# Attention's first query block as one chunk of 128 keys, and the order of logits and result transposes

## The chip, the cores and the metric

The kernel runs on one core of a Trainium2 chip. The metric is the device time of one execution in microseconds (us). A core has TensorE (PE in the profile; its weight loads are PEld), VectorE (DVE), ScalarE (ACT), GpSimd (POOL) and SyncE (SP), which here issues most of the loads and stores. Every engine runs its own queue in the order in which the program was written.

## The reference

Three stages follow one another; only the first is touched by the change.

```
scores = scale * q @ k^T            # batch 4, heads 8, 768 positions, 64 per head
keep   = first 8 keys, or the 96 keys up to the query
scores = where(keep, scores - slope[h] * dist, -1e9)
a      = exp(scores - max);  a = a / (sum(a) + 1e-9)
x      = (a @ v)                    # to 3072 tokens x 512
x      = x + gate * expert(x)       # 8 experts, top 1, only where x @ w_skip > 0
out    = experts by capacity, 384 tokens each (greedy by logits x @ w_gate)
```

## The kernel before

**Attention.** Work goes by batch `b` (4), by pair of heads `hp` (4 each) and by `j` (3), a group of two query blocks of 128 rows, so 16 head pairs of three groups. The loop over `g` is a pipeline written by hand: in one turn it emits the exponentials of group g+2 (`e_stage`), the product with V of group g-1 (`o_stage`), a task or two from the list `todo`, the scaling of group g+1 (`n_stage`), the transposes of probabilities of group g (`t_stage`), the transposes of K and Q of a later pair (`qk_t`) and the scores of group g+3 (`s_stage`).

Only the keys that can count are used: query block i > 0 sees 232 keys (96 before its block, its own 128, the first 8), block 0 sees its own 128. Keys lie on partitions for the product with V, and 232 are more than 128, so every block's keys are split in two by their parity: the exponential writes them de-interleaved (`p r k -> p k r`), and the transposes, the copies and the products with V run over two chunks of half the keys. Block 0 is treated in the same way, with two chunks of 64. V is loaded to match: `vw` for the later blocks, `v0` (the name `v` in the rows) for the first 128 keys, with two neighbouring rows of V on one partition.

Names of tiles: `pb` probabilities, `pP` a bank of PSUM (five rotate) for transposes and more, `pts` the copy of transposed probabilities, `pO` the product with V, `xT` the attention's result with features on partitions, `xs` its transposed copy that is written to memory as `xd` and `x2d`, `pS` scores, `sb` scores with bias, `st` their maxima and sums.

**What stands in `todo`.** After each group but a pair's first, `x_stage` transposes half a pair's result (three transposes). After the last pair of a batch come also `logits` (four products of `xT` with the weights `wc` into `pP`, copied by ScalarE to the single tile `ls`) and `logits_t` (three transposes of `ls`, reduced by VectorE to `LG`). A turn of the loop takes one task, and a second if any is left. When the last batch is done, `route1` ranks the tokens for the first experts; the same routing of earlier batches runs beside the attention, in small VectorE instructions. What is left of `todo` is emitted behind the loop, with work on the expert weights (`ww`) between.

**Experts.** The expert stages follow, from a table of planned costs (`Clock`). They take the rest of the time and are not touched; their instructions and their order stay as they are.

Every operation is recorded through one helper, so all rows of the trace carry its line, L132; pieces are told apart by their tiles.

Of the kernel before, what the change touches and what calls it, by code (L numbers as in the profile page):

```python
# [7 lines left out]
F32 = mybir.dt.float32  # L8
# [162 lines left out]
def tile_attn_moe_moe(ctx: ExitStack, tc: tile.TileContext, q, k, v, n_global, n_local,  # L171
# [93 lines left out]
    def load_v(b, hp):  # L265
        w = VW[b, hp] = ld.tile([KP, NI - 1, 2, 2, D], F32, name="vw", bufs=3)
        z = V0[b, hp] = ld.tile([64, 2, 2, D], F32, name="v0", bufs=3)
        vv = v[b, 2 * hp:2 * hp + 2].rearrange("h (i x) d -> h i x d", x=128)
        nc.sync.dma_start(z.rearrange("p h r d -> p h (r d)"),
                          vv[:, 0].rearrange("h (p r) d -> p h (r d)", r=2))  # L270
        for h in range(2):
            def part(p0, p1, src):
                nc.sync.dma_start(w[p0:p1, :, h].rearrange("p i r d -> p i (r d)"),
                                  src.rearrange("i (p r) d -> p i (r d)", r=2))
            part(W // 2, KP - G // 2, vv[h, 1:])
            part(0, W // 2, vv[h, :NI - 1, 128 - W:])
            part(KP - G // 2, KP, vv[h, 0:1, :G].to_broadcast([NI - 1, G, D]))
# [62 lines left out]

    NG = NI // 2
    GR = [(b, hp, j) for b in range(B) for hp in range(HP) for j in range(NG)]
    SB = {}
# [4 lines left out]
    def s_stage(g):  # L348
# [11 lines left out]
        for x in range(2):  # L360
            i = 2 * j + x
            SB[g, x] = sb = wk.tile([128, 2, KW], F32, name="sb", bufs=4)
            for h in range(2):
                nc.vector.tensor_tensor_reduce(sb[:, h, :keys(i)], p_s[i, h][:, :keys(i)],
                                               (bias1 if i else bias0)[:, 2 * hp + h, :], 1.0, 3e38,
                                               op0=OP.add, op1=OP.min, accum_out=st[:, 0, x, h:h + 1])

    def e_stage(g, x, h):
        n = keys(2 * GR[g][2] + x)
        if h == 0:  # L370
            PB[g, x] = wk.tile([128, 2, 2, KP], F32, name="pb", bufs=6)
        nc.scalar.activation(PB[g, x][:, h, :, :n // 2].rearrange("p r k -> p k r"),
                             SB[g, x][:, h, :n].rearrange("p (k r) -> p k r", r=2), AF.Exp,
                             bias=ST[g][:, 0, x, h:h + 1], scale=-1.0, accum_out=ST[g][:, 1, x, h:h + 1])
        if h == 1:
            SB.pop((g, x))

    def n_stage(g):
# [3 lines left out]
        for x in range(2):  # L382
            n = keys(2 * GR[g][2] + x)
            for h in range(2):
                p = PB[g, x][:, h, :, :n // 2]
                nc.gpsimd.tensor_scalar(p, p, st[:, 2, x, h:h + 1], 1.0, op0=OP.mult, op1=OP.mult)

    def t_stage(g, x):
        n = keys(2 * GR[g][2] + x) // 2
        pt = ps.tile([128, 2, 2, 128], F32, name="pP", bufs=5)  # L390
        p = PB.pop((g, x))
        for h in range(2):
            for r in range(2):
                nc.tensor.transpose(pt[:n, h, r, :], p[:, h, r, :n], ident)
        PT[g, x] = wk.tile([128, 2, 2, 128], F32, name="pts", bufs=3)
        nc.vector.tensor_copy(PT[g, x][:n], pt[:n])

    def o_stage(g):
        b, hp, j = GR[g]
        po = ps.tile([128, 2, 128], F32, name="pO")  # L400
        for x in range(2):
            i = 2 * j + x
            n = keys(i) // 2
            t = PT.pop((g, x))
            for r in range(2):
                for h in (1, 0):
                    vv = VW[b, hp][:, i - 1, h, r, :] if i else V0[b, hp][:, h, r, :]
                    nc.tensor.matmul(po[h * 64:(h + 1) * 64, x, :], vv, t[:n, h, r, :], start=r == 0, stop=r == 1)
        if b not in XT:
# [448 lines left out]
    for g in range(-3, NU + 1):  # L858
# [28 lines left out]
        for i in (2 * j, 2 * j + 1):  # L887
            beside(b, hp, i)
        if j:
            todo.append((x_stage, (b, hp, j - 1)))  # L890
            if hp == HP - 1:
                todo.append((logits, (b, j - 1)))
                todo.append((logits_t, (b, j - 1)))
# [1172 lines left out]
```

## Time and profile before

| | |
|---|---|
| median of 3 runs | 776.23 us (775.8 to 778.62) |
| profiled execution | 777.47 us |
| span of its trace | 775.7 us |
| TensorE busy | 744.8 us, 96% |
| VectorE, ScalarE, GpSimd busy | 68%, 52%, 60% |
| transfers | 145370 packets, 132.23 MB, 170 GB/s |

The span is from the first to the last instruction of the profiled execution; its time, with what lies around, is 1.8 us more. Busy shares are means over stages with different limits, so the stage of the change has to be read by itself. Matmuls overlap in the pipeline: what one costs in a dense stretch is seen from start to start, not from the duration of one.

### The profile page before, as it was taken

Reading aid. Unit: us, or ns where it says so; the run is one execution under the profiler, and the core shown is the slowest. Engines: PE = TensorE matmul, PEld = TensorE weight load, DVE = VectorE, ACT = ScalarE, POOL = GpSimd, SP = SyncE. Lnnn points to the kernel's source line nnn. Section 1 sums busy time; section 2 is a strip of 40 time slices with the busy share of each in tenths; the row PEclk is TensorE's granted clock in tenths of the full one; section 3 lists DMA queues with packets and bytes.
Section 4 is the critical chain, followed back from the end, with each engine's and each line's share of the span. In section 5 each row is a group of like instructions: output and inputs, shape, how many; then the busy total and the mean of one; then the engine's idle time right before and its main releaser. Section 6 shows DMA issues by size and latency. Waiting matters only on the chain.

```text
span 775.7 us, 17432 instructions
## 1 busy us (share of the span) xinstructions
PE 744.8 (96%) x5910; PEld 628.7 (81%) x5910; DVE 526.1 (68%) x1952; ACT 403.3 (52%) x936; POOL 468.2 (60%) x821
## 2 busy tenths in 40 slices
PE   7999999899889999999999999999999999999997
PEld 5887777677659999999888677878788878788986
DVE  5987988979556676777634586778787778752110
ACT  5887787887547655555652113434333434255221
POOL 4664456755214464555793636975768777689911
PEclk9999999999999999999999999999999999999999
DMA  8686988897716766777760035626262636366311
GB/s 192 167 213 167 248 232 200 222 231 199 236 27 213 265 198 195 252 234 224 210 220 33 19 91 191 209 91 222 77 204 84 230 108 206 125 195 185 121 41 41
DMA packets 145370, 132.23 MB, mean 170 GB/s; under 512 B 65427, under 2 KB 112787, under 8 KB 145280
## 3 DMA queue, kind: packets, MB, share of 16 engines
q1 hardware_dynamic: 136896, 111.19, 48.9%
q0 software_dynamic: 6784, 19.51, 7.4%
q8 instruction: 48, 0.79, 0.4%
q10 hardware_dynamic: 1600, 0.39, 0.2%
q14 instruction: 42, 0.34, 0.1%
HBM read 108.80 MB, written 22.79 MB: 170 GB/s over the span
## 4 chain that ended last, share of the span: by engine, by line
PE 44%; POOL 8%; issue 6%; DMA 5%; DVE 4%; ACT 3%; POOLq 0%; DVEq 0%; ACTq 0%; SPq 0%
PE py L132 19%; PE ph L132 19%; POOL wl L132 7%; DMA wr<-in_moe_w_dram 4%; PE pr L132 3%; PE pt L132 3%; ACT wh L132 2%; DVE wl L132 1%; POOL out_dram L132 1%; DMA xg<-x2d,ids 1%; DVE py L132 1%; ACT ya L132 0%; DVE h L132 0%; POOL xg L132 0%; DVE o L132 0%
## 5 line engine op out<-in xcount | busy, mean ns | idle before, releaser
L132 POOL TENSOR_TENSOR wl<-wr,wh 128x256 fp32r<-128x256 f32 x356 | 253.6, 745 | 62.0 <-ACT wh L132 61.3
L132 ACT ACTIVATE wh<-wr 128x1024 fp32r<-128x1024 f32 (+1 forms) x148 | 142.2, 985 | 42.8 <-DMA wr<-in_moe_w_dram 26.8
L132 PE MATMUL py<-wh,h 128*128 128x512 f32 (+1 forms) x448 | 155.9, 401 | 0.0
L132 ACT ACTIVATE h<-ph 128x208 fp32r<-128x208 f32 (+2 forms) x132 | 54.4, 415 | 180.7 <-PE ph L132 168.3
L132 POOL TENSOR_SCALAR pb<-pb,st 128x232 f32<-128x232 f32 (+1 forms) x192 | 83.4, 453 | 74.3 <-ACT pb L132 24.2
L132 ACT ACTIVATE pb<-sb,st 128x232 f32<-128x232 f32 (+1 forms) x192 | 113.8, 664 | 10.1 <-DVE st L132 9.8
L132 DVE SCALAR_TENSOR_TENSOR h<-ph,h 128x208 fp32r<-128x208 f32 (+1 forms) x128 | 58.8, 460 | 88.8 <-ACT h L132 88.7
L132 PE MATMUL ph<-xh,wh 128*128 128x208 f32 (+1 forms) x512 | 99.1, 310 | 1.4 <-DVE h L132 1.4
L132 PE MATMUL ph<-xh,wl 128*128 128x208 f32 (+1 forms) x512 | 100.0, 311 | 0.0
L132 PE MATMUL ph<-xl,wh 128*128 128x208 f32 (+1 forms) x512 | 99.0, 311 | 0.0
L132 PEld LDWEIGHTS py<-wh,h 128*128 128x128 f32 (+1 forms) x448 | 82.0, 185 | 14.1
L132 PE MATMUL py<-wl,h 128*128 128x512 f32 (+1 forms) x224 | 90.9, 406 | 0.0
L132 PEld LDWEIGHTS ph<-xh,wh 128*128 128x128 f32 x512 | 82.2, 190 | 6.8 <-DVE h L132 1.6
L132 PEld LDWEIGHTS ph<-xl,wh 128*128 128x128 f32 x512 | 78.9, 190 | 1.1 <-issue 1.0
L132 PEld LDWEIGHTS ph<-xh,wl 128*128 128x128 f32 x512 | 78.9, 190 | 0.5 <-issue 0.3
L132 DVE TENSOR_TENSOR wl<-wr,wh 128x1024 fp32r<-128x1024 f32 x47 | 61.0, 1304 | 15.3 <-ACT wh L132 15.2
L132 DVE CUSTOM_DVE_ANT_0 sb<-pS,bias 128x232 f32<-128x232 f32 (+1 forms) x192 | 61.4, 374 | 8.9 <-PE pS L132 7.6
L132 DVE COPY pts<-pP 116x512 f32<-116x512 f32 (+1 forms) x96 | 60.7, 672 | 7.6 <-PE pP L132 7.1
L132 POOL DMA_INDIRECT xg<-x2d,ids x24 | 23.8, 990 | 52.2 <-DVE ids L132 19.1
L132 PE MATMUL pS<-kt,qt 64*128 64x232 f32 (+1 forms) x384 | 50.7, 382 | 1.0 <-ACT pb L132 1.0
L132 PE MATMUL pP<-ident,pb 128*116 128x128 f32 (+1 forms) x384 | 51.3, 277 | 0.0
L132 PE MATMUL pO<-pts,vw 116*64 116x128 f32 x640 | 46.3, 281 | 4.0 <-DVE pts L132 3.2
(465 smaller groups left out, 1267.5 us busy)
## 6 DMA issues: line engine op xcount, KB each, us to landing
wr<-in_moe_w_dram SPq DMA_DIRECT2D x136, 512.0 KB
xd<-xs SPq DMA_DIRECT2D x32, 192.0 KB
x2d<-xs SPq DMA_DIRECT2D x32, 192.0 KB
kraw<-in_k_dram SPq DMA_DIRECT2D x30, 192.0 KB
qraw<-in_q_dram SPq DMA_DIRECT2D x30, 192.0 KB
vw<-in_v_dram SPq DMA_DIRECT2D x32, 160.0 KB
vw<-in_v_dram SPq DMA_DIRECT2D x32, 120.0 KB
xT<-in_moe_w_dram SPq DMA_DIRECT2D x1, 1536.0 KB
```

Of the source, the lines that this page charges most:

```text
L132: r = f(*a, **k)
```

## The change

Query block 0 takes its 128 keys as one chunk. Its exponential writes them in one run, a new function `probs` gives the piece of `pb` that holds them, its transposes are one of 128 columns for each head in place of two of 64, the copy to `pts` has 256 elements on 128 partitions in place of 512 on 64, its product with V runs once over 128 rows for each head in place of twice over 64, and V's first block is loaded with one row of 64 numbers (256 bytes) for each partition and head in place of two (512 bytes). The later blocks' `pt` only changes the order of its two inner indices. Apart from that, `logits` goes into `todo` ahead of `x_stage`.

```diff
--- before.py
+++ after.py
@@ -264,10 +264,9 @@
 
     def load_v(b, hp):
         w = VW[b, hp] = ld.tile([KP, NI - 1, 2, 2, D], F32, name="vw", bufs=3)
-        z = V0[b, hp] = ld.tile([64, 2, 2, D], F32, name="v0", bufs=3)
+        z = V0[b, hp] = ld.tile([128, 2, D], F32, name="v0", bufs=3)
         vv = v[b, 2 * hp:2 * hp + 2].rearrange("h (i x) d -> h i x d", x=128)
-        nc.sync.dma_start(z.rearrange("p h r d -> p h (r d)"),
-                          vv[:, 0].rearrange("h (p r) d -> p h (r d)", r=2))
+        nc.sync.dma_start(z, vv[:, 0].rearrange("h p d -> p h d"))
         for h in range(2):
             def part(p0, p1, src):
                 nc.sync.dma_start(w[p0:p1, :, h].rearrange("p i r d -> p i (r d)"),
@@ -339,6 +338,7 @@
 
 
     NG = NI // 2
+    PTS = 3
     GR = [(b, hp, j) for b in range(B) for hp in range(HP) for j in range(NG)]
     SB = {}
 
@@ -365,12 +365,20 @@
                                                (bias1 if i else bias0)[:, 2 * hp + h, :], 1.0, 3e38,
                                                op0=OP.add, op1=OP.min, accum_out=st[:, 0, x, h:h + 1])
 
+    def probs(g, x, h):
+
+        n = keys(2 * GR[g][2] + x)
+        p = PB[g, x][:, h]
+        return p.rearrange("p r k -> p (r k)")[:, :n] if n == 128 else p[:, :, :n // 2]
+
     def e_stage(g, x, h):
         n = keys(2 * GR[g][2] + x)
         if h == 0:
             PB[g, x] = wk.tile([128, 2, 2, KP], F32, name="pb", bufs=6)
-        nc.scalar.activation(PB[g, x][:, h, :, :n // 2].rearrange("p r k -> p k r"),
-                             SB[g, x][:, h, :n].rearrange("p (k r) -> p k r", r=2), AF.Exp,
+        whole = n == 128
+        o_, i_ = probs(g, x, h), SB[g, x][:, h, :n]
+        nc.scalar.activation(o_ if whole else o_.rearrange("p r k -> p k r"),
+                             i_ if whole else i_.rearrange("p (k r) -> p k r", r=2), AF.Exp,
                              bias=ST[g][:, 0, x, h:h + 1], scale=-1.0, accum_out=ST[g][:, 1, x, h:h + 1])
         if h == 1:
             SB.pop((g, x))
@@ -380,32 +388,36 @@
         nc.vector.tensor_scalar(st[:, 2], st[:, 1], 1e-9, None, op0=OP.add)
         nc.vector.reciprocal(st[:, 2], st[:, 2])
         for x in range(2):
-            n = keys(2 * GR[g][2] + x)
             for h in range(2):
-                p = PB[g, x][:, h, :, :n // 2]
+                p = probs(g, x, h)
                 nc.gpsimd.tensor_scalar(p, p, st[:, 2, x, h:h + 1], 1.0, op0=OP.mult, op1=OP.mult)
 
     def t_stage(g, x):
-        n = keys(2 * GR[g][2] + x) // 2
+        n = keys(2 * GR[g][2] + x)
+        nr = 1 if n == 128 else 2
+        n //= nr
         pt = ps.tile([128, 2, 2, 128], F32, name="pP", bufs=5)
-        p = PB.pop((g, x))
         for h in range(2):
-            for r in range(2):
-                nc.tensor.transpose(pt[:n, h, r, :], p[:, h, r, :n], ident)
-        PT[g, x] = wk.tile([128, 2, 2, 128], F32, name="pts", bufs=3)
-        nc.vector.tensor_copy(PT[g, x][:n], pt[:n])
+            p = probs(g, x, h)
+            for r in range(nr):
+                nc.tensor.transpose(pt[:n, r, h, :], p if nr == 1 else p[:, r], ident)
+        PB.pop((g, x))
+        PT[g, x] = wk.tile([128, 2, 2, 128], F32, name="pts", bufs=PTS)
+        nc.vector.tensor_copy(PT[g, x][:n, :nr], pt[:n, :nr])
 
     def o_stage(g):
         b, hp, j = GR[g]
         po = ps.tile([128, 2, 128], F32, name="pO")
         for x in range(2):
             i = 2 * j + x
-            n = keys(i) // 2
+            n = keys(i)
+            nr = 1 if n == 128 else 2
             t = PT.pop((g, x))
-            for r in range(2):
+            for r in range(nr):
                 for h in (1, 0):
-                    vv = VW[b, hp][:, i - 1, h, r, :] if i else V0[b, hp][:, h, r, :]
-                    nc.tensor.matmul(po[h * 64:(h + 1) * 64, x, :], vv, t[:n, h, r, :], start=r == 0, stop=r == 1)
+                    vv = VW[b, hp][:, i - 1, h, r, :] if i else V0[b, hp][:, h, :]
+                    nc.tensor.matmul(po[h * 64:(h + 1) * 64, x, :], vv, t[:n // nr, r, h, :],
+                                     start=r == 0, stop=r == nr - 1)
         if b not in XT:
             XT[b] = wk.tile([128, HP, S], F32, name="xT")
         nc.scalar.activation(XT[b][:, hp, j * 256:(j + 1) * 256], po.rearrange("p a b -> p (a b)"), AF.Copy)
@@ -887,9 +899,10 @@
         for i in (2 * j, 2 * j + 1):
             beside(b, hp, i)
         if j:
+            if hp == HP - 1:
+                todo.append((logits, (b, j - 1)))
             todo.append((x_stage, (b, hp, j - 1)))
             if hp == HP - 1:
-                todo.append((logits, (b, j - 1)))
                 todo.append((logits_t, (b, j - 1)))
                 if j == NG - 1:
                     todo.append((start_r1, (b,)))
```

The piece of TensorE's queue around query block 0 of the second head pair, before (`xT` transposes, `pb` transposes, K and Q, scores, products with V):

```order
L132 MATMUL pP<-ident,xT 128x128 x3
L132 MATMUL pP<-ident,pb 64x128 x4
L132 MATMUL pP<-ident,pb 116x128 x4
L132 MATMUL pP<-ident,kraw 128x128 x2
L132 MATMUL pP<-ident,qraw 128x128 x2
L132 MATMUL pS<-kt,qt 128x232 x2
L132 MATMUL pS<-kt,qt 128x128 x2
L132 MATMUL pO<-pts,v_217 64x128 x4
L132 MATMUL pO<-pts,vw 64x128 x4
```

The same piece with the change:

```order
L132 MATMUL pP<-ident,xT 128x128 x3
L132 MATMUL pP<-ident,pb 128x128 x2
L132 MATMUL pP<-ident,pb 116x128 x4
L132 MATMUL pP<-ident,kraw 128x128 x2
L132 MATMUL pP<-ident,qraw 128x128 x2
L132 MATMUL pS<-kt,qt 128x232 x2
L132 MATMUL pS<-kt,qt 128x128 x2
L132 MATMUL pO<-pts,v_217 64x128 x2
L132 MATMUL pO<-pts,vw 64x128 x4
```

Two transposes and two products fewer, nothing else, in each of the 16 pairs.

TensorE's queue behind the last head pair of the first batch, from its block 0 on, before (`wc` marks the logits, `ls` their transposes):

```order
L132 MATMUL pO<-pts,v_847 64x128 x4
L132 MATMUL pO<-pts,vw 64x128 x4
L132 MATMUL pP<-ident,ls 128x128 x3
L132 MATMUL pP<-ident,xT 128x128 x3
L132 MATMUL pP<-ident,pb 116x128 x8
L132 MATMUL pP<-ident,kraw 128x128 x2
L132 MATMUL pP<-ident,qraw 128x128 x2
L132 MATMUL pS<-kt,qt 128x232 x4
L132 MATMUL pO<-pts,vw 64x128 x8
L132 MATMUL pP<-xT,wc 32x384 x4
L132 MATMUL pP<-ident,ls 128x128 x3
```

With the change:

```order
L132 MATMUL pO<-pts,v_835 64x128 x2
L132 MATMUL pO<-pts,vw 64x128 x4
L132 MATMUL pP<-ident,ls 128x128 x3
L132 MATMUL pP<-xT,wc 32x384 x4
L132 MATMUL pP<-ident,pb 116x128 x8
L132 MATMUL pP<-ident,kraw 128x128 x2
L132 MATMUL pP<-ident,qraw 128x128 x2
L132 MATMUL pS<-kt,qt 128x232 x4
L132 MATMUL pO<-pts,vw 64x128 x8
L132 MATMUL pP<-ident,xT 128x128 x3
L132 MATMUL pP<-ident,ls 128x128 x3
```

The second half's logits and the second half's result transposes have changed places, so a whole turn of the loop now lies between those logits and the transposes that read them. This is so behind the first, second and third batch; behind the fourth, the order of the tasks that are left is changed alike.

SyncE's queue at the same place, before (`LG` logits, `xs` results, then loads of a later pair):

```order
L132 DMA xd<-LG 128x3x8
L132 DMA l2d<-LG 128x3x8
L132 DMA xd<-xs 128x3x128
L132 DMA x2d<-xs 128x3x128
L132 DMA kraw<-in_k_dram 128x6x64 x2
L132 DMA qraw<-in_q_dram 128x6x64 x2
```

With the change, this place and the end of the loads behind it:

```order
L132 DMA xd<-LG 128x3x8
L132 DMA l2d<-LG 128x3x8
L132 DMA kraw<-in_k_dram 128x6x64 x2
L132 DMA qraw<-in_q_dram 128x6x64 x2
L132 DMA v_1255<-in_v_dram 128x2x64
L132 DMA vw<-in_v_dram 64x5x128
L132 DMA vw<-in_v_dram 48x5x128
L132 DMA vw<-in_v_dram 4x5x128
L132 DMA vw<-in_v_dram 64x5x128
L132 DMA vw<-in_v_dram 48x5x128
L132 DMA vw<-in_v_dram 4x5x128
L132 DMA xd<-xs 128x3x128
```

The two writes of these results go behind the eleven loads.

## Rows read from the trace of the kernel before

**Rows 1.** The page: span, and each engine's busy time, share and instructions.

```profile
span 775.7 us, 17432 instructions
PE 744.8 (96%) x5910; PEld 628.7 (81%) x5910; DVE 526.1 (68%) x1952; ACT 403.3 (52%) x936; POOL 468.2 (60%) x821
```

**Rows 2.** Windows of single head pairs: busy PE, PEld, DVE, ACT, POOL; clock, DMA share, GB/s.

```profile
18.50:29.20 10.70, 10.70 (x114) 8.79 (x112) 10.60 (x45) 8.57 (x30) 7.30 (x19) 1.00 0.57 125
29.20:40.23 11.03, 11.03 (x116) 9.12 (x114) 10.53 (x45) 9.43 (x33) 7.02 (x19) 1.00 0.77 199
...
88.33:100.12 11.79, 11.34 (x114) 9.17 (x114) 11.69 (x49) 8.81 (x33) 6.96 (x20) 1.00 0.89 235
100.12:112.06 11.94, 11.94 (x124) 9.24 (x122) 9.52 (x40) 10.16 (x35) 6.95 (x20) 1.00 0.94 249
112.06:125.07 13.01, 12.19 (x127) 9.59 (x126) 9.96 (x41) 10.30 (x35) 8.06 (x20) 1.00 0.86 221
125.07:138.65 13.58, 11.67 (x122) 9.59 (x120) 13.27 (x66) 10.90 (x40) 8.96 (x23) 1.00 0.78 198
...
151.21:163.15 11.94, 11.94 (x125) 9.23 (x123) 10.24 (x41) 11.43 (x41) 10.24 (x25) 1.00 0.91 234
...
188.25:199.24 10.99, 9.72 (x98) 7.63 (x99) 10.79 (x47) 7.89 (x28) 6.16 (x17) 1.00 0.59 173
```

**Rows 3.** Timeline of TensorE in one head pair: start, us, engine, line, operation, count.

```profile
26.98 1.04 PE L132 MATMUL pP<-ident,pb 128*64 128x128 f32 x8
27.86 0.38 PE L132 MATMUL pP<-ident,kraw 128*128 128x128 f32 x2
...
29.20 0.66 PE L132 MATMUL pO<-pts,v 64*64 64x128 f32 x8
29.78 0.66 PE L132 MATMUL pO<-pts,vw 116*64 116x128 f32 x8
30.37 0.55 PE L132 MATMUL pP<-ident,xT 128*128 128x128 f32 x3
30.75 1.04 PE L132 MATMUL pP<-ident,pb 128*116 128x128 f32 x8
31.63 0.38 PE L132 MATMUL pP<-ident,kraw 128*128 128x128 f32 x2
```

**Rows 4.** Timeline of TensorE at both logits behind the second batch's last pair.

```profile
109.03 0.85 PE L132 MATMUL pP<-xT,wc 128*32 128x384 f32 x8
109.82 1.06 PE L132 MATMUL pP<-ident,pb 128*64 128x128 f32 x8
...
117.36 0.85 PE L132 MATMUL pP<-xT,wc 128*32 128x384 f32 x8
119.03 0.55 PE L132 MATMUL pP<-ident,ls 128*128 128x128 f32 x3 [0.82 <-ACT ls L132]
```

**Rows 5.** TensorE's waits, 20 to 212 us: us in total, times, longest.

```profile
PE pO L132 <- DVE pts L132: 3.2, 7, 1.0
PE pP L132 <- ACT ls L132: 2.9, 4, 0.8
```

**Rows 6.** Groups by form, 18 to 232 us: count, busy us, mean ns, idle before.

```profile
L132 DVE COPY kt<-pP 128x256 f32<-128x256 f32 x44 | 18.1, 410 | 0.0
...
L132 DVE COPY pts<-pP 64x512 f32<-64x512 f32 x15 | 9.9, 663 | 3.2 <-PE pP L132 3.1
...
L132 ACT ACTIVATE pb<-sb,st 128x128 f32<-128x128 f32 x30 | 13.5, 514 | 2.2 <-DVE st L132 1.8
...
L132 ACT ACTIVATE wh<-wr 128x256 fp32r<-128x256 f32 x16 | 5.7, 407 | 0.0
```

**Rows 7.** DMA queue in 10:13.5 and in 110.5:113: packets, MB, share of 16 engines.

```profile
q1 hardware_dynamic: 3644, 0.91, 115.5%
...
q1 hardware_dynamic: 1025, 0.50, 69.0%
```

**Rows 8.** Timeline of TensorE where the experts begin.

```profile
232.39 1.65 PE L132 MATMUL py<-ident,xg 128*128 128x128 f32 x8 [2.21 <-issue]
```

**Rows 9.** Window there, columns as in rows 2.

```profile
232.00:234.00 2.00, 1.61 (x9) 1.60 (x10) 0.00 (x0) 0.46 (x1) 1.18 (x2) 0.54 0.46 125
```

## The prediction

> **What bounds the kernel now.** I read the page first. The program lasts 775.7 us on the one core and TensorE is busy in 96% of it [rows 1]. The chain of waits on the page goes back only to about 230 us, where the experts begin, so it is silent on the part that is changed. The attention fills the first 200 us, and for it I cut the trace into windows of one head pair each, from the first product of one pair's query block 0 to that of the next [rows 2]. The reader is to compare three columns with the length of the window: PE, DVE and ACT. There are two kinds of pairs.
>
> In the first kind TensorE has no free time at all: 11.03 busy of 11.03, 11.94 of 11.94. Six of the fifteen windows are so (those at 18.5, 29.2, 40.2, 51.3, 100.1 and 151.2 us), and three more (63.2, 112.1, 163.2 us) are free for one wait only, 0.82 us in the window at 112.06 [rows 2]. VectorE comes next, with 0.1 us free in the window at 18.5 and 0.5 in that at 29.2; ScalarE has over 1.5 us free in these two, but only 0.5 in that at 151.21.
>
> In the second kind VectorE is nearly full: 11.69 of 11.79, 13.27 of 13.58, 10.79 of 10.99 [rows 2]. These six pairs (76.1, 88.3, 125.1, 138.7, 176.1, 188.2 us) carry the first routing's small VectorE instructions. There TensorE waits for the copies of transposed probabilities: 3.2 us in the attention and just behind it [rows 5].
>
> The granted clock is 1.00 in all of these windows, the level of 2.4 GHz.
>
> **The change, part by part.** *Transposes of query block 0.* Four of 64 columns become two of 128. In the timeline eight of them, four of 64 and four of 116 columns, take 0.88 us from their start to that of the next piece (26.98 to 27.86), and eight of 116 columns take 0.88 as well (30.75 to 31.63) [rows 3]. So one costs 0.11 us whatever its columns, and 128 is near 116: two fewer save 0.22 us of TensorE in each head pair.
>
> *Products with V.* Four products over 64 keys become two over 128; in float32 each is two instructions, so eight become four. Eight over 64 rows take 0.58 us (29.20 to 29.78), eight over 116 rows 0.59 (29.78 to 30.37) [rows 3]: 0.073 each, whatever the rows. Four fewer save 0.29 us. The two heads still write different halves of the result's partitions, as with the 116 rows. Together TensorE is 0.51 us shorter in each of 16 pairs, 8.2 us in all.
>
> *The copy of the transposed probabilities.* Its 64x512 elements become 128x256. The first takes 663 ns; another copy out of PSUM, of 128x256, takes 410 [rows 6]. VectorE is 0.25 us shorter in each pair.
>
> *Exponentials and scaling.* ScalarE's exponential over 128 keys now writes one run in place of two interleaved halves. It takes 514 ns now; the upper bound is that it stays so. The nearest ScalarE row with plain runs needs 407 ns for 256 elements [rows 6], so it may fall below 0.4. ScalarE has at least the 0.5 us free that TensorE is to save, so I count nothing for it; in a pair where ScalarE were full, two of them would be worth 0.2 us. GpSimd scales the same 128 elements and is busy 7.02 of 11.03 us: nothing, in either direction.
>
> *The load of V's first block.* 128 packets of 512 bytes become 256 of 256 bytes, in each pair. A stretch in which only packets of about 250 bytes ran shows 3,644 of them in 3.5 us at a share of 115.5% of 16 engines: 17.7 ns each. One of almost only 512 bytes shows 1,025 in 2.5 us at 69.0%: 27 ns each [rows 7]. So the block costs 256 x 17.7 = 4.5 us of engine time, not 3.5, or 0.07 us of the sixteen. The fullest window has a DMA share of 0.94 of 11.94 us, 11.2 us [rows 2]. With 0.07 more this is 11.3, against a pair that would last 11.4. V is loaded two pairs ahead, so I take it as hidden. The Trainium skill speaks against this part: "DMA: Bandwidth & Descriptors", section Specifications, asks for at least 512 bytes and says that shorter transfers are read, modified and written. The trace agrees that they cost more for each byte, 1.3 times. If by that rule the block's traffic doubled (an estimate), it would cost 0.35 us of a pair in place of 0.07; in the fullest pair 0.15 us of that would no longer be hidden, and the sum would be smaller by this for some of the pairs, about 0.5 us in all.
>
> *Logits ahead of transposes.* Before, the second half's logits of a batch run right ahead of the transposes that read them. The logits take 0.79 us where something else follows (109.03 to 109.82), and 1.67 where their transposes follow (117.36 to 119.03) [rows 4]: TensorE waits for ScalarE's copy, 2.9 us in four places in the waits [rows 5]. Now another group's whole work, some 4 us, lies between. This gives 0.88 us at each of three places, 2.6 in all; they lie in the three windows in which TensorE is free for nothing else. At the fourth, behind the last pair, only the result's transposes (0.38 us, from 30.37 to 30.75 [rows 3]) come between; of its share of the waits, some 0.7 us, I take 0.5. Sum: 3.1 us. The wait does not reappear elsewhere: where the logits now stand, the piece ahead of them is the transposes of the earlier logits, which free the single buffer for the copy.
>
> *What moves in the queues.* SyncE's write of the second half's results goes behind eleven loads at three places. The write's tile has two buffers, and the same one is used again about one pair, 12 us, later. I count nothing; were the write not done by then, ScalarE's copy of results would wait, and the exponentials queued behind it, of 0.5 us or more each.
>
> **The sum.** Nine pairs in which TensorE sets the pace: 8 x 0.51, and 0.35 for that at 18.5 us, where VectorE has 0.10 free and gains 0.25: 4.4 us. Six in which VectorE sets it: 0.25 from the copy and about 0.1 of its free time, 0.35 each: 2.1 us. The first pair's transposes, ahead of these windows and beside the first loads, and the last pair's products behind them: between 0 and 0.5, I take 0.4. Logits: 3.1 us. In all 10.0 us. Everything behind hangs on the attention's end: the last logits are ranked, the ids gathered, and TensorE begins the experts after 2.2 us of issue [rows 8]. I expect that part to move as one block. The profiled execution took 777.47 us, 1.8 more than its span, and would take 767.5; the median shown is 776.23, 1.2 lower, so I predict 766.2 us. What this kernel's measurement can tell from no change is about 0.5%, 3.9 us.
>
> **The rivals.** *VectorE or ScalarE paces everywhere* once TensorE is faster. For it: in the window at 29.2 us VectorE would have 10.28 of 10.52 us, little for a queue that is served in order. Against it: TensorE has no gap there now. Then a pair gains only the copy's 0.25 us, 4 us in 16, and the logits' wait only half: 5.5 in all, 770.7 us.
>
> *The logits' move gives nothing*, because ScalarE's copies are only done in another order and its queue is what TensorE waits for. For it: ScalarE is busy 10.30 us in the window at 112.06, more than in most [rows 2]. Against it: the wait named is the copy of the logits itself. Gain 7 us, 769.2.
>
> *More than the sum*: all 16 pairs give the 0.51 us, since copies that come 0.25 us sooner from transposes 0.22 us sooner also shorten the waits of 3.2 us [rows 5]. That is 8.2 + 3.1, and one to two of the waits: 12 to 13, about 764.
>
> *DMA becomes the bound, and the kernel slower.* Place: the pairs from 76 to 176 us, where a pair's DMA work is up to 11.2 us. For it: smaller packets, and a stage that asks for the same bytes in less time. Point of decision: the mean packet must cost 20% more, so that 11.2 becomes 13.4 us. Then eight pairs last 1.5 us longer, 12 in all, and the rest gains 7: +5, 781 us. Against it: no wait of TensorE for a load is among its waits, and the 256-byte packets of K and Q, the bulk, show 17.7 ns.
>
> A last unknown is the granted clock where the experts begin: 0.54 over two us after that idle time [rows 9], part at 1.2 GHz. A shifted program can meet this sooner, later or not at all; 1.5 us either way.
>
> **How the numbers follow.** The forecast, 8.5 to 11.5 us gained, has a chance of 0.50. VectorE's pace has 0.22, the logits without effect 0.13, more than the sum 0.09, DMA 0.04; 0.02 is left for a gain under 3.9 us otherwise. Of VectorE's pace a quarter ends within 0.5%. So faster has 0.88, no change 0.08, slower 0.04. For eight in ten the range leaves out DMA, the top of "more" and the weak half of VectorE's pace: 764 to 771.5 us. The forecast alone is 764.7 to 767.7.
>
> **What would show it.** Windows of one pair without routing should last 10.5 us in place of 11.03, with TensorE still full; VectorE's copy of 128x256 should take about 0.41 us; the logits' transposes should follow without a wait at the three places; TensorE should begin the experts near 222.4 us, not 232.4. I am wrong if pairs keep their length with TensorE now idle (VectorE's pace), if waits for loads appear, or if the experts begin ten us sooner and the end doesn't move.

## The result, and the profile after

The changed kernel takes 768.03 us (766.85 to 768.44, 4 runs) against 776.54 us (775.8 to 778.62, 4 runs) for the kernel before on the same chip: a ratio of 0.9878, interval 0.9859 to 0.9897. The gain is 8.5 us where 10.0 was forecast. In two more comparisons on other chips the ratio was 0.988 (0.9862 to 0.9899) and 0.987 (0.9847 to 0.9894).

The page of the changed kernel, span and first row of busy times; the profiled execution took 768.39 us:

```profile
span 766.6 us, 17242 instructions
PE 738.0 (96%) x5814; PEld 622.2 (81%) x5814; DVE 523.2 (68%) x1952; ACT 402.2 (52%) x936; POOL 468.3 (61%) x821
```

TensorE has 96 matmuls fewer (two transposes and four product instructions in 16 pairs) and 6.8 us less busy time. The span is 9.1 us shorter, so some waits went too. The head pairs show where. Windows of single pairs after the change, cut and laid out as [rows 2]:

```profile
28.75:39.20 10.45, 10.45 (x110) 8.72 (x108) 10.35 (x45) 9.41 (x33) 6.96 (x19) 1.00 0.71 181
...
84.59:96.20 11.61, 11.02 (x109) 8.79 (x109) 11.51 (x49) 8.96 (x33) 7.00 (x21) 1.00 0.97 256
96.20:107.43 11.23, 11.23 (x118) 8.87 (x116) 9.35 (x40) 10.34 (x38) 7.17 (x21) 1.00 0.95 247
107.43:119.14 11.71, 11.71 (x121) 9.18 (x120) 9.65 (x41) 10.04 (x35) 8.30 (x20) 1.00 0.89 228
119.14:132.08 12.94, 11.27 (x115) 9.15 (x114) 12.45 (x65) 10.71 (x39) 8.46 (x22) 1.00 0.84 222
...
179.23:189.79 10.56, 9.40 (x93) 7.24 (x93) 10.46 (x47) 7.74 (x29) 5.95 (x17) 1.00 0.65 184
```

The two kinds of pairs of [rows 2] are still there. In the windows that begin at 28.75, 96.20 and 107.43 TensorE is still full and the pair is 0.58, 0.71 and 1.30 us shorter than its counterpart before. In those at 84.59, 119.14 and 179.23 VectorE is still nearly full (0.1, 0.5 and 0.1 us free), TensorE has 0.6 to 1.7 us free, and the gain is only 0.18, 0.64 and 0.43.

The pieces of TensorE in the pair of [rows 3], after:

```profile
26.75 0.82 PE L132 MATMUL pP<-ident,pb 128*128 128x128 f32 x6
27.41 0.38 PE L132 MATMUL pP<-ident,kraw 128*128 128x128 f32 x2
...
28.75 0.44 PE L132 MATMUL pO<-pts,v 128*64 128x128 f32 x4
29.02 0.61 PE L132 MATMUL pO<-pts,vw 116*64 116x128 f32 x8
29.56 0.55 PE L132 MATMUL pP<-ident,xT 128*128 128x128 f32 x3
```

From start to start, six transposes take 0.66 us (26.75 to 27.41) where eight took 0.88, four products 0.27 where eight took 0.58, and the eight products of the next query block, which the change doesn't touch, 0.54 where they took 0.59. The place of the second logits of [rows 4], after:

```profile
112.96 0.55 PE L132 MATMUL pP<-ident,xT 128*128 128x128 f32 x3
113.35 0.49 PE L132 MATMUL pP<-ident,ls 128*128 128x128 f32 x3
113.67 1.04 PE L132 MATMUL pP<-ident,pb 128*116 128x128 f32 x8
```

The transposes of `ls` follow without a wait. The groups by form that answer to [rows 6] (VectorE's copy, ScalarE's exponential):

```profile
L132 DVE COPY pts<-pP 128x256 f32<-128x256 f32 x15 | 6.0, 402 | 2.2 <-PE pP L132 2.2
...
L132 ACT ACTIVATE pb<-sb,st 128x128 f32<-128x128 f32 x30 | 11.8, 395 | 2.5 <-DVE st L132 1.4 <-POOL pb L132 0.7
```

TensorE's waits from 20 to 203 us, to be held against [rows 5], and then one row of ScalarE's in the same stretch:

```profile
PE pO L132 <- DVE pts L132: 3.5, 8, 1.0
PE pO L132 <- ACT pb L132: 1.6, 4, 1.1
```

```profile
ACT xs L132 <- DMA x2d<-xs: 2.2, 2, 2.1
```

The 2.9 us for `ls` are gone, the 3.2 for VectorE's `pts` are still there (3.5). A third row, for ScalarE's exponentials (`pb`), is now 1.6 us. The kernel before had it too (20 to 212 us), and the prediction did not read it:

```profile
PE pO L132 <- ACT pb L132: 2.8, 4, 1.3
```

ScalarE's waits name the write of `xs`, for which the prediction counted nothing; the last experiments are about it. The experts begin here:

```profile
222.85 0.93 PE L132 MATMUL py<-ident,xg 128*128 128x128 f32 x8 [2.21 <-issue]
```

That is 9.54 us earlier than in [rows 8]; of this 0.4 is lost again behind it.

### The profile page after: what moved, and what is told of

Read it like the earlier page. It is cut to its first block, busy times and chain, and to the rows that moved or that the text cites. A ratio compares the mean times of both kernels' runs of the same rounds, so it can differ in the third digit from the quotient of the medians.

```text
span 766.6 us, 17242 instructions
## 1 busy us (share of the span) xinstructions
PE 738.0 (96%) x5814; PEld 622.2 (81%) x5814; DVE 523.2 (68%) x1952; ACT 402.2 (52%) x936; POOL 468.3 (61%) x821
## 4 chain that ended last, share of the span: by engine, by line
PE 41%; POOL 13%; issue 8%; DMA 4%; DVE 3%; ACT 2%; POOLq 0%; DVEq 0%; ACTq 0%; SPq 0%
PE py L132 18%; PE ph L132 18%; POOL wl L132 11%; PE pr L132 3%; DMA wr<-in_moe_w_dram 3%; PE pt L132 2%; ACT wh L132 1%; POOL out_dram L132 1%; DMA xg<-x2d,ids 1%; DVE wl L132 1%; POOL xg L132 1%; DVE py L132 1%; ACT ya L132 0%; DVE o L132 0%; DVE gm L132 0%
## 5 line engine op out<-in xcount | busy, mean ns | idle before, releaser
L132 DVE COPY pts<-pP 116x512 f32<-116x512 f32 (+1 forms) x96 | 57.0, 631 | 6.4 <-PE pP L132 6.3
L132 PE MATMUL pP<-ident,pb 128*116 128x128 f32 (+1 forms) x352 | 48.3, 277 | 0.9 <-DVE gate L132 0.9
```

What stands on the lines that cost most here:

```text
L132: r = f(*a, **k)
```

## The experiments

The theory: TensorE paces nine pairs and VectorE six; the parts add up; transfers are hidden. Its rivals: VectorE paces all pairs, the logits' move is worth nothing, or the transfers are not hidden. The ratios are to the kernel before on the same chip, with 95% intervals; the chips differ (medians of the kernel before from 776.5 to 784.2 us), so times of different groups are not compared. The four of the first group ran on one chip, and so on.

### First group: the two halves, the products' price, and the change once more

**e1_logits_only** is the kernel before with this part alone:

```diff
+            if hp == HP - 1:
+                todo.append((logits, (b, j - 1)))
             todo.append((x_stage, (b, hp, j - 1)))
             if hp == HP - 1:
-                todo.append((logits, (b, j - 1)))
                 todo.append((logits_t, (b, j - 1)))
```

> The kernel before with only the order of todo changed (logits ahead of the transposes of results). Theory: the wait of 0.82 us for ScalarE's copy goes at three places, the head pairs with logits fall from 13.0 to 12.2 us, 2.5 us in all, some 774 us; the tail behind the last pair gives 0.1 at most, as in the changed kernel. Rival (ScalarE's queue is what TensorE waits for): the same total as before, 776.5. All pairs without logits keep their length (11.03 and so on).

**e2_chunk_only** is the changed kernel with that part undone.

> The changed kernel with the old order of todo, so the one chunk of 128 keys alone. Theory: the pairs without logits stay as in the changed kernel (10.45 us for the second), those with logits are 0.8 us longer and show the wait for the copy of the logits again: 2.5 us more than 768.0, 770.5. Rival (the logits' move gives nothing): 768. If the gains of 0.6 to 0.7 us in the pairs that TensorE paces, where 0.51 was forecast, have to do with the new order, they fall back here to 0.5.

**e3_products_twice**:

```diff
-                for h in (1, 0):
+                for h in (1, 0) if i else (1, 0, 1, 0):
```

> The changed kernel with each of block 0's two products with V done twice, the second time over the first with the same result: four products for a pair as before, TensorE's 0.27 to 0.29 us given back and nothing else. Theory: the pairs that TensorE paces are 0.27 us longer (10.45 becomes 10.7), the six that VectorE paces under 0.1; with the logits' pairs 2.5 to 3 us in all, 770.5 to 771. Rival (VectorE paces all pairs): under 0.5 us in all, 768.0 to 768.5.

**e0_after_again** has no edit.

> The changed kernel again, for its time beside the others on one chip and a second trace: 768.0 us. If the 0.45 us by which the expert part grew and the place of the low clock (near 488 us in place of 232) belong to the program, both are found again; if they are chance, they differ.

Measured: 774.38 us, ratio 0.9955 (0.9938 to 0.9972) for the logits alone; 770.62, 0.9906 (0.9889 to 0.9923) for the chunk alone; 771.22, 0.9911 (0.9891 to 0.9931) with the products twice; 767.5, 0.988 (0.9862 to 0.9899) for the changed kernel. 0.45% and 0.94% make 1.4% where both together gave 1.2%: within the intervals they add up. The intervals of e2_chunk_only and e3_products_twice touch that of the changed kernel, so what follows rests on the traces. The lengths of six pairs, from the windows of each trace, by their start in the kernel before:

| pair at | before | changed | logits alone | chunk alone | products twice |
|---|---|---|---|---|---|
| 40.23 | 11.04 | 10.45 | 11.04 | 10.46 | 10.67 |
| 100.12 | 11.94 | 11.23 | 11.82 | 11.39 | 11.45 |
| 112.06 | 13.01 | 11.71 | 12.26 | 12.48 | 11.93 |
| 76.07 | 12.26 | 12.00 | 12.26 | 12.00 | 12.00 |
| 88.33 | 11.79 | 11.61 | 11.79 | 11.61 | 11.61 |
| 188.25 | 10.99 | 10.56 | 12.00 | 10.57 | 11.55 |

The first three are TensorE's. Twice the products cost each of them 0.22 us; the same work costs the pairs at 76.07 and 88.33 nothing. That is the theory's pattern, and VectorE as the pace of all pairs is refuted: then no pair would have become longer. The logits alone take 0.12 us from the pair at 100.12 and 0.75 from that at 112.06, 0.87 together, as the 0.88 of the prediction has it; without the move the wait is back. TensorE in e2_chunk_only:

```profile
113.09 0.85 PE L132 MATMUL pP<-xT,wc 128*32 128x384 f32 x8
114.79 0.55 PE L132 MATMUL pP<-ident,ls 128*128 128x128 f32 x3 [0.84 <-ACT ls L132]
```

One pair doesn't fit: that at 188.25 lost 1.0 us with the logits alone (against the kernel before) and with the products twice (against the changed one). So part of the total that I forecast for e3_products_twice came from a pair for which nothing was forecast. The last group returns to it. The second trace of the changed kernel also answers on the experts. Windows of e0_after_again at the two places (the eighth number is the granted clock):

```profile
223.00:225.00 2.00, 2.00 (x13) 1.56 (x12) 1.09 (x2) 1.84 (x4) 0.90 (x1) 0.50 0.55 146
488.00:490.00 2.00, 2.00 (x10) 1.69 (x10) 1.79 (x12) 2.00 (x4) 2.00 (x4) 1.00 0.02 6
```

and the same two windows of the changed kernel's first trace:

```profile
223.00:225.00 2.00, 2.00 (x20) 1.79 (x19) 0.83 (x2) 1.46 (x3) 1.46 (x2) 1.00 0.35 75
488.00:490.00 2.00, 2.00 (x7) 1.62 (x6) 1.83 (x12) 1.86 (x4) 2.00 (x3) 0.50 0.74 229
```

The same program has the lower level (1.2 GHz) at 223 us in one run and at 488 in the other, each time behind idle time of TensorE: 2.21 us before 222.2, or 1.92 before 487.1 for gathered rows. The same 2.21 us stand ahead of the full clock in the other trace, so idle time alone doesn't decide it, and its place is not the change's doing.

### Second group: VectorE's copy, the packets, the buffers of xs

**e4_copy_scalar**:

```diff
-        nc.vector.tensor_copy(PT[g, x][:n, :nr], pt[:n, :nr])
+        if nr == 1:
+            nc.scalar.activation(PT[g, x][:n, 0], pt[:n, 0], AF.Copy)
+        else:
+            nc.vector.tensor_copy(PT[g, x][:n, :nr], pt[:n, :nr])
```

> The changed kernel with block 0's copy of transposed probabilities (128x256, 0.40 us) done by ScalarE in place of VectorE; all else alike. Theory (VectorE's work paces the six pairs with routing): these are 0.3 to 0.4 us shorter, 2 us in all, 765.5 to 766; the pairs that TensorE paces keep 10.45 and 11.23. Rival (the place in the queues counts, not VectorE's busy time): no pair becomes shorter, 767.5 to 768. A loss is possible in the one pair where ScalarE is full (11.24 of 11.24 us): 0.2 to 0.4 us.

**e5_v_packets**:

```diff
-        nc.sync.dma_start(z, vv[:, 0].rearrange("h p d -> p h d"))
+        for d in (0, 32):
+            nc.sync.dma_start(z[:, :, d:d + 32], vv[:, 0].rearrange("h p d -> p h d")[:, :, d:d + 32])
```

> The changed kernel with V's first block loaded as two transfers of 32 columns: 512 packets of 128 bytes a pair in place of 256 of 256 bytes, one load more on SyncE's queue. Theory (the loads are hidden): no pair changes by over 0.1 us, 767.5 to 768. Rival (DMA is near its bound in the fullest pairs, so that smaller packets cost): at 17.7 ns a packet 0.28 us more in the eight pairs from 72 to 167 us, 2 us, 770.

**e6_xs_three**:

```diff
-        xs = wk.tile([128, 3, 128], F32, name="xs", bufs=2)
+        xs = wk.tile([128, 3, 128], F32, name="xs", bufs=3)
```

> The changed kernel with three buffers for the transposed results (xs) in place of two, all instructions the same. ScalarE's wait for the write of xs (2.2 us and 5.4 us in the two traces) should be gone. Theory A: TensorE has slack there, so nothing is gained, 767.5 to 768. Theory B: the wait delays the exponentials behind it, and the pairs after a batch's end (the tenth and eleventh) are 0.2 us shorter each, 767.2.

**e7_both** has the edits of e4_copy_scalar and e6_xs_three.

> The changed kernel with both: block 0's copy on ScalarE and three buffers for xs. Theory: the two add up; 2 us from the copy, 0 to 0.5 from the buffers, 765.2 to 766. Rival: as the changed kernel, 767.5 to 768.

Measured: ratios 0.9931 (0.9911 to 0.9952) for the copy on ScalarE, 0.994 (0.9917 to 0.9964) for the packets, 0.9886 (0.9859 to 0.9914) for three buffers and 0.9923 (0.9894 to 0.9952) for both edits. The changed kernel itself did not run in this group; on three other chips it had 0.987 to 0.988. Three buffers alone are level with that: ScalarE's waits for the write of `xs` are gone from the pairs, and no pair is clearly shorter. The copy and the packets lost 0.45 and 0.54% against the 0.9886; their intervals lie close to that of three buffers (0.9911 and 0.9917 against 0.9914) and clear of those of the changed kernel. My theory's number for the copy (2 us faster) was wrong, and so was that for both edits: the third buffer does not give the copy's loss back. TensorE's waits in e4_copy_scalar, 18 to 200 us, and then ScalarE's and TensorE's rows at one of them:

```profile
PE pO L132 <- ACT pts L132: 5.1, 9, 1.4
PE pO L132 <- DVE pts L132: 1.6, 4, 0.4
```

```profile
27.36 0.68 ACT L132 ACTIVATE pb<-sb,st 128x232 f32<-128x232 f32 x1
...
27.91 0.37 ACT L132 ACTIVATE pts<-pP 128x256 f32<-128x256 f32 x1
...
28.33 0.44 PE L132 MATMUL pO<-pts,v 128*64 128x128 f32 x4 [0.25 <-ACT pts L132]
```

VectorE was relieved, its waits halved, but the copy now stands between ScalarE's exponentials and came later: 5.1 us of waits for it in nine places. The pair at 40 us is 0.1 longer, that at 28 us 0.4, and none of the six became shorter than in the changed kernel's first trace; over the fifteen windows 175.1 us stand against 171.5 to 172.1 in its three. With the third buffer in e7_both ScalarE waits for no write there, and the pair at 28 us still takes 10.83 in place of 10.45, so the loss is not that write's. An engine's free time doesn't say when it would serve one more instruction; its queue does.

### Third group: VectorE's routing spread, and the packets again

**e8_route_spread**, at seven places of `route1`:

```diff
-        yield 0.5
+        yield 3.5
```

(one of the seven had 2.5).

> The changed kernel with the steps of the first routing, beside the attention, one a turn of the loop in place of one a query block, so that VectorE's small instructions spread over some 2.7 pairs in place of 1.5; the same instructions in all. Theory (VectorE's work, in its order, paces the six pairs): TensorE waits there 4.9 us in all now (12.00 against 11.34 busy, 11.61 against 11.02, 12.94 against 11.27, 12.39 against 11.02, 11.82 against 11.21); at least 1.5 us of this goes, and the eighth and twelfth pairs (11.23) stay as they are, since VectorE has 1.4 to 1.9 us free in them: 2 to 3 us faster than the changed kernel on this chip. Rival (these pairs wait for something else, ScalarE or the transfers of 0.9 share): no change within 0.5 us.

**e9_after_third** is the changed kernel.

> The changed kernel once more, for the two beside it on the same chip: the attention to the first product of the last pair at 189.3 to 189.8 us as twice before, the part of the experts between 542.8 and 543.7 us if the differences between the kernels there (542.8 to 547.5) come with the kernel, wider if they are chance.

**e10_v_packets_again** is the kernel of e5_v_packets.

> The kernel with V's first block in packets of 128 bytes again. Its attention was as long as the changed kernel's, pair by pair, yet its runs were 0.5% slower, all of it in the part of the experts, which has the same instructions. Theory (chance of that chip and its traces: waits for gathered rows, and the low clock): now level with the changed kernel, within 0.3%. Rival (the smaller packets do cost, by a way that the attention's windows don't show): 0.5% slower again.

Measured: ratio 0.9887 (0.9859 to 0.9914) for the routing spread, 0.987 (0.9847 to 0.9894) for the changed kernel, 0.9945 (0.9922 to 0.9968) for the packets. Five windows of e8_route_spread, the pairs that begin at 72.6, 84.6, 96.2, 119.1 and 144.5 us in the changed kernel:

```profile
71.15:82.91 11.76, 11.27 (x116) 9.15 (x114) 11.09 (x60) 9.18 (x35) 6.70 (x20) 1.00 0.92 233
82.91:93.92 11.01, 10.78 (x110) 8.76 (x109) 10.63 (x55) 9.21 (x35) 5.16 (x16) 1.00 0.97 261
93.92:105.55 11.63, 11.52 (x116) 8.92 (x116) 10.54 (x43) 10.26 (x36) 7.93 (x23) 1.00 0.92 248
...
117.26:129.40 12.14, 11.51 (x115) 9.20 (x114) 11.64 (x56) 9.80 (x36) 8.95 (x23) 1.00 0.87 232
...
142.15:154.03 11.88, 11.67 (x117) 8.93 (x117) 11.53 (x43) 10.23 (x36) 10.17 (x25) 1.00 0.89 222
```

Pairs that were relieved are shorter: 12.00 becomes 11.76, 11.61 becomes 11.01, and 12.94 to 13.27 becomes 12.14. So the routing's instructions do set the length of these pairs. But the pairs to which they moved are longer, 11.63 and 11.88 where the changed kernel has 11.23, though VectorE had 1.4 to 1.9 us free in them, and one more of the six is longer too (12.75 where it has 12.2 to 12.4). Over the fifteen windows 171.2 us stand against 172.1 in e9_after_third: 0.9 us, not the 2 to 3 forecast, and nothing that the medians show. VectorE and TensorE of e8_route_spread where the lengthened pair at 93.92 begins:

```profile
92.26 0.95 DVE L132 TENSOR_TENSOR ohs<-slot,ri 128x768 bf16<-128x768 bf16 x1
...
93.42 0.99 DVE L132 COPY pts<-pP 128x256 f32<-128x256 f32 x2
```

```profile
93.92 0.44 PE L132 MATMUL pO<-pts,v 128*64 128x128 f32 x4
94.47 0.73 PE L132 MATMUL pO<-pts,vw 116*64 116x128 f32 x8
```

An instruction of the routing (`ohs`, 0.95 us) now stands ahead of the two copies. They end at 94.41, and the second product begins at 94.47, 0.55 us behind the first; in the changed kernel the copies end ahead of both products, and the second follows after 0.27. It is the same lesson as with the copy: an instruction set ahead of `pts` in a queue served in order delays the products, whether or not the engine is full.

The packets lost again, 0.75% this time, so it was no chance of one chip. The rival of the expectation is true in that they cost. Two things about this edit have to be kept in mind. It makes the packets smaller and also adds a load to SyncE's queue in each pair (1.1 us of issuing for V's first block in place of 0.6); no run parts the two. And the expectation overlooked one pair: in e5_v_packets that before the last took 11.08 us in place of 10.57. The second trace shows more there. ScalarE and TensorE in e10_v_packets_again, in the pair before the last:

```profile
186.73 0.49 ACT L132 ACTIVATE xs<-pP 128x384 f32<-128x384 f32 x1 [4.67 <-DMA x2d<-xs]
188.21 0.37 ACT L132 ACTIVATE qt<-pP 128x256 f32<-128x256 f32 x1
188.68 1.92 PE L132 MATMUL pS<-kt,qt 64*128 64x232 f32 x8 [2.41 <-issue]
```

ScalarE's copy of results waits 4.67 us for its buffer, whose earlier content is still to be written to memory. Behind it in ScalarE's queue stand two exponentials and the copy `qt`, and TensorE's scores begin when `qt` is done. The profile calls that wait "issue", since the releaser isn't seen. SyncE ahead of it, and then in the changed kernel at the same place (a merged row runs from the start of its first issue to the end of its last):

```profile
174.73 0.46 SPq L132 DMA_DIRECT2D xT<-in_moe_w_dram  x1
175.23 1.12 SPq L132 DMA_DIRECT2D v<-in_v_dram  x2
176.47 7.22 SPq L132 DMA_DIRECT2D vw<-in_v_dram  x6
183.78 0.38 SPq L132 DMA_DIRECT2D xd<-xs  x1
```

```profile
171.25 0.47 SPq L132 DMA_DIRECT2D xT<-in_moe_w_dram  x1
171.76 0.61 SPq L132 DMA_DIRECT2D v<-in_v_dram  x1
172.47 3.79 SPq L132 DMA_DIRECT2D vw<-in_v_dram  x6
179.34 0.38 SPq L132 DMA_DIRECT2D xd<-xs  x1
```

The pair begins at 179.78 here and at 179.23 there, so the write of `xs` is issued 4.0 us behind its start in place of 0.1. What holds it is named by SyncE's own waits, in the kernel before (184 to 190 us), the changed one (176 to 180) and e10_v_packets_again (178 to 184):

```profile
SPq L132 <- DMA xT<-in_moe_w_dram: 4.6, 1, 4.6
```

```profile
SPq L132 <- DMA xT<-in_moe_w_dram: 3.0, 1, 3.0
```

```profile
SPq L132 <- DMA xT<-in_moe_w_dram: 3.3, 1, 3.3
```

This is one load of expert weights, 1536 KB, into a buffer of `xT` that has come free. In the trace SyncE's transfers bear eight completion marks in turn, and the write of `xs` bears that of this load, eight transfers earlier. In all fourteen traces SyncE sends the next transfer with that mark within 0.1 us of the load's landing. In the changed kernel SyncE has issued all loads of V by 176.26, the load of `xT` lands at 179.28, and the write goes out at 179.34. With the packets SyncE issues that load 5.0 us ahead of the pair in place of 8.0, and it lands at 183.41; the mark now falls on the last load of V, just ahead of the write. So 3.3 of the 7.22 us of that row are a wait, and not the loads' own time. Why SyncE comes to the load of `xT` later there isn't shown. The Trainium skill ("DMA: Bandwidth & Descriptors", section "Queues, rings and completion order") says that each DMA engine takes a sequencer's transfers in the order of its ring; this write was late before it reached a ring, so this trace doesn't test that.

### Fourth: the packets with a third buffer

**e11_v_packets_xs_three** has the edits of e5_v_packets and e6_xs_three.

> V's first block in packets of 128 bytes, and three buffers for the transposed results xs. Theory: the smaller packets cost through the write of xs alone, which stands behind the loads on SyncE's queue (ScalarE waited 8.1 us for it in the last trace, and the pair before the last took 13.73 us in place of 10.57); with a third buffer that wait is gone, this pair takes 10.6 us again, and the ratio to the kernel before is that of the changed kernel, 0.987 to 0.989. Rival (smaller packets slow something else too, such as the part of the experts): the ratio stays at 0.994.

Measured: ratio 0.9868 (0.9847 to 0.9889), that of the changed kernel. The pair before the last, in e10_v_packets_again and in e11_v_packets_xs_three:

```profile
179.78:193.52 13.74, 10.83 (x93) 8.45 (x93) 10.75 (x47) 8.38 (x30) 6.70 (x19) 0.88 0.78 219
```

```profile
179.22:189.79 10.57, 9.40 (x93) 7.24 (x93) 10.46 (x47) 7.85 (x29) 5.99 (x17) 1.00 1.04 297
```

With a third buffer, 1.5 KB a partition, the packets of 128 bytes and their additional load cost nothing measurable. So they don't bind by the engines' time; the loss needs the two buffers of `xs`, and the path that the trace shows is the late write. The write itself is no earlier here: the load of `xT` lands 5.0 us behind the pair's start, later than the 3.6 of e10_v_packets_again, and the pair is as short as in the changed kernel.

How much of the loss took this path is less sure. The traced run of e10_v_packets_again is 2.6 us longer than that of e9_after_third, which the 3.2 us of this pair cover; but it is one of the shorter of nine. Five took 780.2 to 781.7 us at a mean clock of 0.989 to 0.991 (the other four 0.991 to 0.995), and none of these was traced. In the traced run of e5_v_packets, a short one too, the pair lost 0.5 us, yet the experts begin when they do in e6_xs_three (222.69 us), and the 2.4 us by which it is longer lie behind that. That the untraced runs lose by the same write is inferred from the third buffer alone, which ran four times, on another chip.

The write also accounts for the misfit of the first group. In this pair, the later the load of `xT` lands, the longer ScalarE waits, and the longer the pair (all with the chunk; e4_copy_scalar and e8_route_spread, which change these pairs otherwise, are left out):

| trace | load of `xT` lands, us behind the pair's start | ScalarE's wait for `x2d<-xs`, us | the pair, us |
|---|---|---|---|
| chunk alone | -0.1 | 0.67 | 10.57 |
| changed, first and third trace | 0.1, 0.1 | 2.08, 2.17 | 10.56, 10.57 |
| changed, second trace | 1.1 | 2.76 | 10.82 |
| packets, first trace | 2.0 | 3.04 | 11.08 |
| products twice | 2.8 | 3.51 | 11.55 |
| packets, second trace | 3.6 | 4.67 | 13.74 |

Up to some 2.2 us nothing is lost; above, TensorE waits too (part of the last row is the clock of 0.88). With the logits alone the load lands 2.9 us behind the start, the wait is 3.62 and the pair 12.00 where the kernel before has 10.99. These last are read from single traces and not tested with a third buffer. Two more pairs have such a wait in some traces, with other loads ahead of the write. In that at 88.33 in the kernel before it is at most 0.9 us and costs nothing. In that at 138.65 ScalarE waits 0 to 2.6 us in the other traces of the table without any lengthening, and only the 3.46 us of e10_v_packets_again go with a longer pair (13.03 in place of 12.2 to 12.4).

## Why the prediction was right

*Transposes*: 0.22 us a pair forecast, 0.22 measured (0.88 to 0.66).

*Products with V*: 0.29 forecast, 0.31 measured; 0.05 more came from the eight products behind. The pairs that TensorE alone paces gained 0.58 where 0.51 was forecast. The step that was mis-sized is "0.073 each, whatever the rows": done twice, the four instructions cost only 0.22 us a pair, 0.055 each. So an instruction repeated on the same shape costs less than the first ones did; why, I didn't test.

*Copy and exponential*: the copy takes 402 ns, forecast as 410; the exponential 395, just below the 0.4 us that was left open.

*The six pairs of VectorE*: 2.1 us forecast, 2.04 measured in the first trace (0.26 + 0.18 + 0.64 + 0.17 + 0.36 + 0.43); 1.8 and 1.7 in the two others. The number held as a sum, and this is partly luck: 0.35 was forecast for each, and they gained 0.17 to 0.64. The idea behind it, VectorE's busy time, is only half right, as e4_copy_scalar and e8_route_spread show: what counts is what stands ahead of `pts` in its queue. Nor do these pairs wait for `pts` alone, as the prediction has it: the longest wait there, 1.35 us ahead of the product at 138.65, is named for ScalarE's `pb`. What stands behind that name I didn't test.

*The nine pairs of TensorE, with three of the logits*: 4.4 + 2.6 = 7.0 forecast, 7.2 measured (7.1 and 7.0 in the other traces). In parts: with the chunk alone eight pairs gain 0.53 to 0.59 each, where 0.51 was forecast; the one at 18.5 us gains 0.04 to 0.21 where 0.35 was; the logits give 2.4 to 2.5. The rival "logits give nothing" is refuted by e1_logits_only.

*The tail*: 0.5 for the fourth logits forecast. From the last pair's first products to the experts it took 33.15 us before and 33.06, 32.93 and 33.07 after: 0.1 to 0.2. The first transposes of `ls` in it do come sooner, 8.72 us behind those products before and 8.34, 8.21 and 8.34 after. But the second ones come after 12.35 us before and 12.25, 12.12 and 12.25 after, and the experts follow them by 20.8 us in all four traces. So 0.4 to 0.5 us were won at the first wait, and 0.3 were lost again before the second transposes. Between the two TensorE has the same pieces in another order; what loses the time isn't shown. This step was over-sized by 0.3 to 0.4.

*Experts as one block*: they began 9.5 us sooner; their own part took 543.3 us before, and 543.7, 542.8 and, on another chip, 549.1 after. The 0.4 us that the first trace gave back are within what two runs of one program differ by. So "one block" holds, with a wider spread than I had allowed: 1.5 us for the clock alone was too little.

*SyncE's queue*: "I count nothing" held in the time, by luck more than by reasoning. The moved writes themselves make nobody wait in the first trace: none of ScalarE's copies in the pair that follows a batch's logits is late. The wait comes two pairs later, where the order of the queue is the old one, and the kernel before has it too, under another name: at 192.29 us its copy to `xs` waits 1.77 us and the row names TensorE's scores. Its trace has the earlier write complete at 192.13, 0.16 us ahead of that copy, and in the changed kernel it is 183.42 and 183.58. With the old order the wait is 1.77 and 0.67 us, with the new one and packets of 256 or 512 bytes 2.0 to 3.6 in seven traces. Whether the new order lengthens it, or the pairs that follow faster, is open: I made no kernel that parts the two. What the prediction had right is the way the loss takes: ScalarE's copy first, then the exponentials queued behind it. What it had wrong is what would make the write late: it looked at the eleven loads, and the write waits for one load of 1536 KB.

*The packets*: that 256 bytes are hidden held (chunk alone, pairs as forecast). The Trainium skill's limit of 512 bytes for transfers at full rate ("DMA: Bandwidth & Descriptors", section Specifications) shows here only as time for each byte: the median packet of 128, 256 and 512 bytes took 13, 18 and 27 ns between 20 and 190 us. No doubling of traffic is seen in these times.

*The sum*: 9.1 us between the two profiled executions, in place of 10.0: the nine pairs +0.2, the six -0.1, the start -0.2, the tail -0.4, the experts -0.4. The medians differ by 0.6 less, 8.5. All of it lies in the range.

## What to carry to other kernels

Cut the trace into the loop's own periods and ask for each which engine is full: work taken from TensorE paid in full in eight periods of fifteen and in part in seven, and which they are could be read before. Free time of an engine is no promise: a copy moved to an engine with time free came later and cost 0.5%, since it queued behind others. A store must be followed both ways: back to what its queue waits for ahead of it, here the landing of one large load, and on to the buffer that it frees and to everything queued behind the next writer of that buffer. One more buffer is cheap insurance against a load that lands late.

## What was not expected of the hardware

V's first block in packets of 128 bytes and two loads, by 13 ns a packet 2 us of engine time more a pair, or 0.13 us of the sixteen, made a kernel 0.54 and 0.75% slower, and in a run on one more chip a third buffer of another tile left nothing of it. TensorE's waits name no transfer there. The store was held 3 us in the changed kernel by the landing of a load issued eight transfers earlier, 8.0 us after its issue. The part of the experts, the same instructions in every kernel, took 542.8 us in one trace of the changed kernel and 549.1 in another on another chip.
